# Carrying the sign of a weight through a leaky activation while float64 weights are converted

## The chip, the cores and the metric

The kernel runs on one core of a Trainium2 chip. The metric is the device time of one execution in microseconds (us), as the median of the runs shown. The engines are TensorE (PE, with its weight loads shown as PEld), VectorE (DVE), ScalarE (ACT), GpSimd (POOL) and the queues that start transfers, SyncE (SP) above all.

## The reference

Attention with a learned bias over positions (4 batches, 8 heads, 576 positions, head size 64) is followed by a feed-forward layer on 2304 tokens. The second part is the one that matters here:

```python
def _moe_ref(x, w_in, w_out):          # x: 2304 x 512, w_in: 512 x 2048, w_out: 2048 x 512
    h = x @ w_in
    beta = 1.0
    neg = h <= -beta
    pos = h >= beta
    g = np.where(pos, h, np.where(neg, 0.0, (h + beta) ** 2 / (4.0 * beta)))
    return (g @ w_out).astype(np.float32)
```

The two weight matrices arrive as float64. Everything else arrives as float32.

## The kernel before

Three stages follow each other. Stage one builds the position bias (the first third of the span). Stage two runs 16 steps of attention, one per pair of heads and batch; step 15 is the last. Stage three is the feed-forward layer, in three blocks of 768 tokens. A block runs over 16 slices f of the 2048 hidden columns, and each slice over two halves j of 384 tokens. For one slice and one half, `up_proj` issues 12 matmuls into a PSUM tile `h` (lines L731 to L733), `act` turns `h` into the gate (below), and `down_proj` issues 9 matmuls (L752 to L754) that add to six PSUM tiles `y`. There are two `h` tiles in all, so the up-projection two halves later writes into the tile that `act` has to have read.

`act` is a chain over three engines: VectorE clamps `h` into `c` (L740), ScalarE squares it (L741), VectorE takes the larger of `h` and `c` (L742), which frees the `h` tile, ScalarE rounds the result to `gh` (L743) and GpSimd forms the rest `gl` (L744). Values are kept as a high and a low part, since a product on TensorE takes shortened operands; hence three matmuls for each product.

During block 0 the weights are converted as well. Each slice has two tiles of 128 x 512 values, `wi` and `wo`, named `rawi`/`ai` and `rawo`/`ao` on the way, 32 tiles in all. `weight` does one: SyncE loads the 64-bit words into `raw` (L109); ScalarE turns the upper half of each word's low part into the three bits that float32 takes from it (L114, written back into `raw`); ScalarE scales the absolute value of the high part, read as a float32, by 2^-112 into `a` (L115), which rebases the exponent; VectorE shifts that left by three and joins the three bits (L116); VectorE masks the sign out of the high part and joins it (L117); ScalarE rounds to the high part of the weight (L119) and GpSimd forms the low part (L120). The `raw` buffer can be loaded again once its last reader is done, which is L117. From slice 2 on, all `wo` tiles take turns in one buffer and all `wi` tiles in two.

The tokens `x` of a half are loaded by eight transfers on SyncE (L438 twice, L447 six times, fewer where a piece is whole), then multiplied and split on VectorE and ScalarE (L461, L462, L463, L467). `xh0_1_1` below is token block 0, row group 1, half 1. Four such loads, for half 1 of block 0, stand between the attention and the feed-forward layer's full pace.

The order of the instructions on each engine is set when the program is built: a scheduler merges the stages from what it reckons each instruction costs, and every engine then works its list strictly in order. A waiting instruction holds up all that stands behind it on its engine. The functions print below with the profile's line numbers.

Of the kernel before, what the change touches and what calls it, by code (L numbers as in the profile page):

```python
# [8 lines left out]
F32 = mybir.dt.float32  # L9
# [3 lines left out]
AF = mybir.ActivationFunctionType  # L13
ALU = mybir.AluOpType
# [35 lines left out]
def attn_cpb_moe_kernel(ctx, tc, qk, vL, cb, win, wout, lw, dd, ident, ii, out):  # L50
    nc = tc.nc
# [42 lines left out]
    def raw_pool():  # L94
        turn[0] += 1
        return rps[turn[0] % len(rps)]
# [8 lines left out]
    def weight(src, dst, name):  # L105

        rp = raw_pool()
        raw = rp.tile([P, DM, 2], I32, tag="raw", name=f"raw{name}")
        nc.sync.dma_start(out=raw.rearrange("p a b -> p (a b)"), in_=src.bitcast(I32))  # L109
        a = rp.tile([P, DM], F32, tag="a", name=f"a{name}")  # L110
        t = a.bitcast(I32)
        lo, hi = raw[:, :, 0], raw[:, :, 1]

        nc.scalar.activation(lo, raw.bitcast(U16).rearrange("p a (b c) -> p a b c", c=2)[:, :, 0, 1], AF.Identity, scale=2.0**-13, bias=floor_s)  # L114
        nc.scalar.activation(a, hi.bitcast(F32), AF.Abs, scale=2.0**-112)  # L115
        nc.vector.scalar_tensor_tensor(out=t, in0=t, scalar=3, in1=lo, op0=ALU.logical_shift_left, op1=ALU.bitwise_or)  # L116
        nc.vector.scalar_tensor_tensor(out=t, in0=hi, scalar=-0x80000000, in1=t, op0=ALU.bitwise_and, op1=ALU.bitwise_or)  # L117
        h, l = dst
        nc.scalar.copy(h, t.bitcast(F32))  # L119
        nc.gpsimd.tensor_tensor(out=l, in0=t.bitcast(F32), in1=h.bitcast(F32), op=ALU.subtract)  # L120

    def weights(f):
        weight(win[f], [x.rearrange("p a b -> p (a b)") for x in wi[f]], f"i{f}")
        weight(wout[f * P : f * P + P], wo[f], f"o{f}")
# [752 lines left out]
```

## Time and profile before

| | us |
|---|---|
| median of 3 runs | 824.17 (823.49 to 824.81) |
| the profiled execution, whole | 826.46 |
| span of its trace | 824.7 |
| TensorE busy in the span | 733.7 (89%) |
| VectorE busy | 522.7 (63%) |
| ScalarE busy | 468.9 (57%) |
| GpSimd busy | 420.6 (51%) |

The trace starts at 0 and ends at 824.7; attention ends near 391, the weights are converted from 367 to 524, block 0 ends near 549. Busy shares over the whole span say little, since the stages have different limits; the rows further down are cut to the stretch in which the weights are converted. A row of a timeline gives the start, the length, the engine, the line and the tiles, and in brackets how long the engine had been idle before and what ended that. "PEclk" is the granted clock of TensorE, 1.00 being 2.4 GHz and 0.50 being 1.2 GHz.

### The profile page before, as it was taken

How to read it: one execution, taken by the hardware profiler on the slowest of the kernel's cores; microseconds unless marked ns; L12 is line 12 of the kernel's file. 1: busy time of each engine (PE TensorE's matmuls, PEld its weight loads, DVE VectorE, ACT ScalarE, POOL GpSimd, SP SyncE). 2: the span in 40 equal slices, each digit the busy share in tenths (PEclk: the TensorE clock that was granted, in tenths of full speed). 3: DMA queues.
4: the chain of work that ended last, by engine and by line, in shares of the span. 5: the costliest groups of instructions: out<-in, count | busy, mean ns of one | idle time of the engine just before them, and what ended most of it. 6: DMA issues, size and time to landing. Idle time of an engine off the chain costs nothing. (4 is left out here: it accounts for less than half of the span.)

```text
span 824.7 us, 13466 instructions
## 1 busy us (share of the span) xinstructions
PE 733.7 (89%) x4692; PEld 645.4 (78%) x4692; DVE 522.7 (63%) x1053; ACT 468.9 (57%) x1014; POOL 420.6 (51%) x385
## 2 busy tenths in 40 slices
PE   2766779899989999987499889999999999999998
PEld 1232579898989989976387778899999999999996
DVE  8999858788768888866598867366322234222222
ACT  1986758698878888777477854443222233222222
POOL 5875667778767878873176654422222222222221
PEclk9967989999999999998799999999999999999999
DMA  6676787866796587536654455035100012000002
GB/s 192 181 205 200 197 193 198 253 176 169 196 243 177 149 233 172 127 82 168 202 172 161 154 144 156 26 105 171 32 1 1 1 29 76 1 1 1 1 0 78
DMA packets 58660, 103.60 MB, mean 126 GB/s; under 512 B 12496, under 2 KB 32608, under 8 KB 58592
## 3 DMA queue, kind: packets, MB, share of 16 engines
q1 hardware_dynamic: 44976, 83.08, 35.2%
q0 software_dynamic: 2304, 9.96, 5.9%
q10 hardware_dynamic: 11312, 9.70, 3.8%
q8 instruction: 37, 0.61, 0.3%
q14 instruction: 31, 0.25, 0.1%
HBM read 67.63 MB, written 25.12 MB: 112 GB/s over the span
## 5 line engine op out<-in xcount | busy, mean ns | idle before, releaser
L744 POOL TENSOR_TENSOR gl<-c,gh 128x384 fp32r<-128x384 f32 x96 | 103.5, 1078 | 241.9 <-ACT gh L743 212.4
L731 PE MATMUL h<-xh,wi 128*128 128x384 f32 x384 | 133.7, 348 | 21.6 <-DVE c L742 13.8
L741 ACT ACTIVATE c<-c,half_s 128x384 f32<-128x384 f32 x96 | 59.1, 615 | 162.4 <-DVE c L740 162.4
L740 DVE TENSOR_SCALAR c<-h 128x384 f32<-128x384 f32 x96 | 53.2, 554 | 138.9 <-PE h L733 138.9
L732 PE MATMUL h<-xl,wi 128*128 128x384 f32 x384 | 131.5, 342 | 0.8 <-POOL xl L465 0.7
L733 PE MATMUL h<-xh,wi 128*128 128x384 f32 x384 | 131.6, 343 | 0.3 <-POOL wi L120 0.3
L558 POOL TENSOR_TENSOR lo<-c,hi 128x512 fp32r<-128x512 f32 x75 | 100.8, 1349 | 60.8 <-DVE hi L557 57.9
L754 PE MATMUL y<-wo,gl 128*128 128x512 f32 x288 | 114.0, 396 | 0.0
L753 PE MATMUL y<-wo,gh 128*128 128x512 f32 x288 | 113.7, 395 | 0.0
L752 PE MATMUL y<-wo,gh 128*128 128x512 f32 x288 | 112.0, 389 | 0.0
L511 DVE CUSTOM_DVE_ANT_0 e<-S,bias 128x576 f32<-128x576 f32 x128 | 93.9, 746 | 21.8 <-PE S L509 21.5
L518 ACT ACTIVATE e<-e,mx 128x576 f32<-128x576 f32 x128 | 99.7, 780 | 4.0 <-DVE mx L511 1.9
L731 PEld LDWEIGHTS h<-xh,wi 128*128 128x128 f32 x384 | 73.7, 192 | 32.8 <-DVE c L742 20.0
L508 PE MATMUL S<-kh,qa 128*128 128x288 f32 x256 | 80.2, 329 | 19.0 <-DMA kh<-kh 7.6
L742 DVE TENSOR_TENSOR c<-h,c 128x384 f32<-128x384 f32 x96 | 53.4, 556 | 52.4 <-ACT c L741 52.4
L743 ACT CAST gh<-c 128x384 fp32r<-128x384 f32 x96 | 49.2, 513 | 53.4 <-DVE c L742 50.9
L732 PEld LDWEIGHTS h<-xl,wi 128*128 128x128 f32 x384 | 73.8, 192 | 5.3 <-POOL xl L465 1.0
L573 PE MATMUL T<-id_s,e 128*128 128x128 f32 x512 | 73.3, 276 | 2.0 <-ACT e L518 1.4
L733 PEld LDWEIGHTS h<-xh,wi 128*128 128x128 f32 x384 | 73.6, 192 | 0.6 <-POOL wi L120 0.5
L509 PE MATMUL S<-ls,qa 128*128 128x288 f32 x256 | 73.0, 302 | 0.0
L508 PEld LDWEIGHTS S<-kh,qa 128*128 128x128 f32 x256 | 49.0, 191 | 26.9 <-DVE mx L511 11.5
L573 PEld LDWEIGHTS T<-id_s,e 128*128 128x128 f32 x512 | 61.2, 142 | 3.2 <-ACT e L518 1.7
(143 smaller groups left out, 1583.8 us busy)
## 6 DMA issues: line engine op xcount, KB each, us to landing
bias_d<-y SPq DMA_DIRECT2D x36, 295.5 KB, 3.2
qk<-in_qk_dram SPq DMA_DIRECT2D x16, 608.0 KB
qa<-in_qk_dram POOLq DMA_DIRECT2D x16, 608.0 KB, 6.6
x<-xT SPq DMA_DIRECT2D x48, 192.0 KB, 3.7
rawi<-in_win_dram SPq DMA_DIRECT2D x16, 512.0 KB, 3.8
rawo<-in_wout_dram SPq DMA_DIRECT2D x16, 512.0 KB, 4.1
v<-in_vL_dram SPq DMA_DIRECT2D x16, 320.0 KB, 3.2
qa<-ls SPq DMA_DIRECT2D x32, 152.0 KB, 3.8
```

The costliest lines, as they stand in the source:

```text
L508: nc.tensor.matmul(ps[:, hf, :HS], qs[:, qc], kh[:, kc : kc + HS], start=True, stop=False)
L511: nc.vector.tensor_tensor_reduce(out=ev.rearrange("p (a b) -> p a b", a=2), in0=ps[:, :, :HS], in1=bias[k][:, S * j : S * j + S].rearrange ...
L518: lambda ev=ev, j=j: nc.scalar.activation(ev, ev, AF.Exp, bias=mx[:, j : j + 1], scale=-1.0, accum_out=sm[:, 4 * j + k : 4 * j + k + 1])
L558: r = nc.gpsimd.tensor_tensor(out=lo, in0=m, in1=hi.bitcast(F32), op=ALU.subtract)
L573: nc.tensor.transpose(ps[:, tb, :], e[:, c0 : c0 + P], id_s)
L731: nc.tensor.matmul(ps[:, :TH], wh_, xh, start=k == 0, stop=False)
L732: nc.tensor.matmul(ps[:, :TH], wh_, xl, start=False, stop=False)
L733: nc.tensor.matmul(ps[:, :TH], wl_, xh, start=False, stop=k == NK - 1)
L744: nc.gpsimd.tensor_tensor(out=gl, in0=c, in1=gh.bitcast(F32), op=ALU.subtract)
L752: nc.tensor.matmul(y, gh[:, c], wo[f][0], start=f == 0, stop=False)
L753: nc.tensor.matmul(y, gh[:, c], wo[f][1], start=False, stop=False)
L754: nc.tensor.matmul(y, gl[:, c], wo[f][0], start=False, stop=f == NF - 1)
```

## The change

L115 becomes a leaky function: for a positive value it still gives the value times 2^-112, and for a negative one that times -(2^32), which is positive and has the exponent field raised by 32, one bit (bit 28) that is otherwise clear. The shift by three in L116 moves that bit to bit 31, the sign. L117 goes away, and with it 32 instructions on VectorE (1050 rows of its list become 1018). Nothing reads the high part of `raw` after L115, and L116 is the last reader of `raw`. Later lines move up by one (L742 is L741 in the changed program).

```diff
         nc.scalar.activation(lo, raw.bitcast(U16)..., AF.Identity, scale=2.0**-13, bias=floor_s)
-        nc.scalar.activation(a, hi.bitcast(F32), AF.Abs, scale=2.0**-112)
+        nc.scalar.activation(a, hi.bitcast(F32), AF.Prelu, scale=2.0**-112, alpha=-(2.0**32))
         nc.vector.scalar_tensor_tensor(out=t, in0=t, scalar=3, in1=lo, op0=ALU.logical_shift_left, op1=ALU.bitwise_or)
-        nc.vector.scalar_tensor_tensor(out=t, in0=hi, scalar=-0x80000000, in1=t, op0=ALU.bitwise_and, op1=ALU.bitwise_or)
         h, l = dst
```

Since the scheduler merges by cost, the lists of all engines change between the end of the attention and the last weight. TensorE's list has the same 4564 rows and differs in nine short places, all between the last attention step and slice 2 of block 0.

VectorE's list, in slices 3 and 4 of block 0 (`c4_0` is `c` of slice 4, half 0; `ai7` is weight tile `wi` of slice 7), before:

```order
L742 TENSOR_TENSOR c3_1_6210<-h3_1_6188,c3_1_6210 128x384
L117 SCALAR_TENSOR_TENSOR ai7_6328<-rawi7_6326,ai7_6328 128x512
L116 SCALAR_TENSOR_TENSOR ai8_6406<-ai8_6406,rawi8_6404 128x512
L117 SCALAR_TENSOR_TENSOR ai8_6406<-rawi8_6404,ai8_6406 128x512
L740 TENSOR_SCALAR c4_0_6240<-h4_0_6218 128x384
L116 SCALAR_TENSOR_TENSOR ao5_6181<-ao5_6181,rawo5_6179 128x512
L117 SCALAR_TENSOR_TENSOR ao5_6181<-rawo5_6179,ao5_6181 128x512
L742 TENSOR_TENSOR c4_0_6240<-h4_0_6218,c4_0_6240 128x384
```

The same place in the changed program:

```order
L741 TENSOR_TENSOR c3_1_6198<-h3_1_6176,c3_1_6198 128x384
L116 SCALAR_TENSOR_TENSOR ai7_6314<-ai7_6314,rawi7_6312 128x512
L739 TENSOR_SCALAR c4_0_6228<-h4_0_6206 128x384
L116 SCALAR_TENSOR_TENSOR ai8_6390<-ai8_6390,rawi8_6388 128x512
L741 TENSOR_TENSOR c4_0_6228<-h4_0_6206,c4_0_6228 128x384
```

Between the two joins of `c` (L742, now L741) six instructions became three: the three L117 are gone, and one L116 on either side moved past the joins.

SyncE's list, at the loads of the token half 1 of block 0 (`x0_0_1` and `x0_1_1`) and of the weights `rawi1` and `rawo1`, before:

```order
L447 DMA x0_0_1_5867<-rT0_1_75 64x192
L109 DMA rawi1_5702<-in_win_dram 128x1024
L447 DMA x0_0_1_5867<-rT0_1_75 64x192
L438 DMA x0_1_1_5882<-xT1_0_65 64x2x384 x2
L447 DMA x0_1_1_5882<-rT1_0_78 64x128 x2
L447 DMA x0_1_1_5882<-rT1_0_78 64x64 x2
L447 DMA x0_1_1_5882<-rT1_1_79 64x192
L109 DMA rawo1_5711<-in_wout_dram 128x1024
L447 DMA x0_1_1_5882<-rT1_1_79 64x192
```

The same place in the changed program:

```order
L109 DMA rawi1_5700<-in_win_dram 128x1024
L446 DMA x0_0_1_5863<-rT0_1_75 64x192 x2
L437 DMA x0_1_1_5878<-xT1_0_65 64x2x384 x2
L446 DMA x0_1_1_5878<-rT1_0_78 64x128 x2
L109 DMA rawo1_5708<-in_wout_dram 128x1024
L446 DMA x0_1_1_5878<-rT1_0_78 64x64 x2
L446 DMA x0_1_1_5878<-rT1_1_79 64x192 x2
```

The weight loads moved forward: behind `rawi1` stand two token loads of `x0_0_1` instead of one, and behind `rawo1` four of `x0_1_1` instead of one.

ScalarE's list, in slice 7, where the first tokens of block 1 are rounded (`xh768_0_0`), before:

```order
L119 CAST wi0_15_5860<-ai15_6952 128x512
L741 ACTIVATE c7_1_6522<-c7_1_6522,half_s_113 128x384
L463 CAST xh768_0_0_7039<-x768_0_0_7032 128x384
L743 CAST gh7_1_6523<-c7_1_6522 128x384
L114 ACTIVATE rawo10_6569<-rawo10_6569,floor_s_115 128x512
```

The same place in the changed program:

```order
L118 CAST wi0_15_5856<-ai15_6922 128x512
L118 CAST wo0_10_5838<-ao10_6550 128x512
L462 CAST xh768_0_0_7007<-x768_0_0_7000 128x384
L740 ACTIVATE c7_1_6502<-c7_1_6502,half_s_113 128x384
L742 CAST gh7_1_6503<-c7_1_6502 128x384
```

The square of `c7_1` moved from ahead of `xh768_0_0` to behind it.

## Rows read from the trace of the kernel before

**Rows 1.** The page's table of 40 slices, VectorE's busy tenths.

```profile
DVE  8999858788768888866598867366322234222222
```

**Rows 2.** Busy us of each engine by stretch: PE, PEld, DVE, ACT, POOL, PEclk, DMA.

```profile
400.00:440.00 40.00, 31.40 (x138) 27.36 (x139) 32.19 (x42) 27.08 (x48) 21.09 (x16) 0.83 0.56 179
440.00:480.00 40.00, 34.78 (x161) 29.83 (x160) 31.75 (x40) 28.19 (x50) 28.84 (x21) 0.96 0.46 149
480.00:525.00 45.00, 41.47 (x203) 35.95 (x203) 31.25 (x50) 24.85 (x44) 20.29 (x18) 1.00 0.49 138
560.00:824.70 264.70, 260.67 (x1304) 235.30 (x1302) 83.16 (x146) 75.32 (x135) 62.77 (x62) 1.00 0.09 27
```

**Rows 3.** TensorE's waits, 396 to 409, 409 to 480, 480 to 525: us, times, longest.

```profile
PE h L731 <- ACT xh L463: 6.7, 2, 3.5
...
PE h L731 <- DVE c L742: 8.6, 7, 3.1
...
PE h L731 <- DVE c L742: 3.5, 4, 2.2
```

**Rows 4.** VectorE's timeline, 409 to 411 and 436 to 443.5.

```profile
409.74 0.68 DVE L117 SCALAR_TENSOR_TENSOR ai<-rawi,ai 128x512 int32<-128x512 int32 x1
...
436.59 0.55 DVE L742 TENSOR_TENSOR c<-h,c 128x384 f32<-128x384 f32 x1
437.06 0.68 DVE L117 SCALAR_TENSOR_TENSOR ai<-rawi,ai 128x512 int32<-128x512 int32 x1
437.66 0.68 DVE L116 SCALAR_TENSOR_TENSOR ai<-ai,rawi 128x512 int32<-128x512 int32 x1
438.37 1.40 DVE L117 SCALAR_TENSOR_TENSOR ai<-rawi,ai 128x512 int32<-128x512 int32 x1
439.69 0.55 DVE L740 TENSOR_SCALAR c<-h 128x384 f32<-128x384 f32 x1
440.16 1.32 DVE L116 SCALAR_TENSOR_TENSOR ao<-ao,rawo 128x512 int32<-128x512 int32 x1
441.52 1.64 DVE L117 SCALAR_TENSOR_TENSOR ao<-rawo,ao 128x512 int32<-128x512 int32 x1
443.08 0.54 DVE L742 TENSOR_TENSOR c<-h,c 128x384 f32<-128x384 f32 x1
```

**Rows 5.** TensorE's timeline at 443.68.

```profile
443.68 0.69 PE L731 MATMUL h<-xh,wi 128*128 128x384 f32 x1 [2.02 <-DVE c L742]
```

**Rows 6.** TensorE alone, 444 to 447: busy us, PEclk, DMA.

```profile
444.00:447.00 3.00, 3.00 (x10) 0.50 0.51 175
```

**Rows 7.** L117 alone on VectorE, by stretch: busy us (count), PEclk, DMA.

```profile
400.00:480.00 80.00, 24.49 (x22) 0.89 0.51 164
480.00:525.00 45.00, 5.65 (x6) 1.00 0.49 138
```

**Rows 8.** ScalarE's groups: busy us, mean ns of one, idle before.

```profile
L518 ACT ACTIVATE e<-e,mx 128x576 f32<-128x576 f32 x128 | 99.7, 780 | 4.0 <-DVE mx L511 1.9 <-DMA v<-in_vL_dram 0.9 <-ACT ai L115 0.7
...
L548 ACT CAST hi<-T 128x512 fp32r<-128x512 f32 x53 | 29.0, 580 | 6.9 <-PE S_L L530 4.9 <-PE T L573 2.0
...
L115 ACT ACTIVATE ai<-rawi 128x512 f32<-128x512 f32 x16 | 10.7, 668 | 0.0
...
L239 ACT ACT_TABLE_LOAD x1 | 1.3, 1283 | 4.9 <-DMA lw_s<-in_lw_dram 4.9
```

**Rows 9.** SyncE's timeline at the two weight loads.

```profile
383.12 0.34 SPq L109 DMA_DIRECT2D rawi<-in_win_dram  x1
...
390.27 0.33 SPq L109 DMA_DIRECT2D rawo<-in_wout_dram  x1
390.64 0.44 SPq L447 DMA_DIRECT2D x<-rT  x1
```

**Rows 10.** L120 on GpSimd, 405 to 525: duration ns min/median/max.

```profile
L120 POOL TENSOR_TENSOR wi<-ai,wi x14: 1270/1470/1843, 411.4 to 478.9; 128x512 fp32r<-128x512 f32 x14
```

**Rows 11.** ScalarE's timeline at the first tokens of block 1.

```profile
480.17 0.51 ACT L463 CAST xh<-x 128x384 fp32r<-128x384 f32 x1 [2.24 <-POOL wi L120]
```

## The prediction

> **What bounds the kernel now.** I read the table of slices first, then cut the span into stretches. After 560 TensorE is busy 260.67 of 264.70 us [rows 2]: nothing that VectorE does there can shorten the time, and no conversion is left there. From 400 to 480 it is another engine's turn: VectorE is busy 32.19 and 31.75 of 40 us, while TensorE stands idle 8.6 and 5.2 us and ScalarE and GpSimd are lighter than both [rows 2]. The page shows the same hump in VectorE's slices 18 to 23 [rows 1]. What TensorE waits for there is one thing: the join of `c` on VectorE (L742), 8.6 us in seven waits from 409 to 480 and 3.5 us in four waits from 480 to 525. Ahead of that, 6.7 us in two waits go to the tokens of half 1 [rows 3].
>
> Why the join is late is seen in one gap. TensorE starts at 443.68 after 2.02 us idle [rows 5]. VectorE had run without a pause from 436.59: between two joins stand L117, L116, L117, the clamp, L116, L117 [rows 4]. Three of the six are L117, and they hold 0.68, 1.40 and 1.64, together 3.7 us, more than the gap. So L117 lies on the path here, though it belongs to weights that are needed only slices later.
>
> **The change, part by part.** *L117 leaves VectorE.* From 400 to 480 that is 22 instructions and 24.49 us, from 480 to 525 six and 5.65 us [rows 7]. VectorE's load from 400 to 480 falls from 63.9 to 39.4 of 80 us [rows 2, 7]. That is an engine's time, not the kernel's: only what ends in a TensorE gap counts. Four terms follow.
>
> First, the gap before 410.94, the longest of the seven with 3.1 us [rows 3]. The join there stands behind one L117 of 0.68 [rows 4]; the rest is the chain from a late matmul through clamp and square. Credit 0.7.
>
> Second, the other six waits up to 480: 8.6 - 3.1 = 5.5 us. In the changed list the place of the 443.68 gap keeps only two L116 and the clamp between the joins, so 3.7 us leave against 2.02 of gap, and this gap should close. Not every gap will, since lists in order jar also without a full engine. The nearest measure is 480 to 525, where VectorE is busy 31.25 of 45 us [rows 2], with three waits of 3.5 - 2.2 = 1.3 us beside the long one [rows 3]. At that rate the 68 us from 412 to 480 keep 1.3 / 39 x 68 = 2.3 us. Credit 5.5 - 2.3 = 3.2; bounds 0 and 5.5.
>
> Third, the clock. Right after the 2.02 us gap TensorE ran at 0.50, the lower of its two levels, for the 3 us from 444 to 447 [rows 6], which is 1.5 us of work lost. If the gap closes, so should that dip. Credit 1.5; bounds 0 and 1.5.
>
> Fourth, 480 to 525: 3.5 us in four waits. The long one, 2.2, starts with ScalarE, which waited 2.24 us to round `xh768_0_0` until GpSimd was done with the last `wi` tile [rows 11]. The changed list keeps that wait, and even puts the square of `c7_1` behind it; I credit it one L117 of 0.68 and no more. The other three are 1.3 us, and an L117 there lasts 5.65 / 6 = 0.94 us [rows 7]; I credit half, 0.7. Together 1.4; bounds 0 and 3.5.
>
> *L115 becomes a leaky function.* The trace of before has no such operation. ScalarE's rows on tiles of this kind lie between 580 ns (a rounding of 512 columns) and 780 ns (the exponential, 576 columns); the absolute value takes 668 [rows 8]. It keeps its place and its scale, so I take the 668 of the nearest row, no change. The ends are -0.09 and +0.11 us a tile, times 22 tiles -2 and +2.5 us on ScalarE, which is busy 55.3 of 80 us [rows 2] and has room for either. It costs nothing under the time in which TensorE works; if ScalarE filled up, it would cost its whole length (a rival below).
>
> *The raw buffer is free one instruction earlier.* Before, SyncE could start the next load only behind L117; now behind L116. So weights come earlier, which speeds nothing by itself, as TensorE never waits for a `wo` in these rows [rows 3]. *Queues are shifted by that.* SyncE started `rawi1` at 383.12 and `rawo1` at 390.27 [rows 9], each after an L117. Now each can start up to one L117 earlier (0.68 to 1.64 [rows 4]), but two and four token loads stand behind them instead of one and one. One such issue takes 0.44 [rows 9] and they follow each other: with `rawo1` 1.6 us earlier and three loads more behind it (3 x 0.44 = 1.3, more where an issue is slower) `x0_1_1` is complete at about the same time as before. If `rawo1` doesn't start earlier, the tokens slip by 1.3 to 2 us and TensorE's second token wait grows by as much. I take 0; bounds -0.8 and +2.
>
> *One rule of contention.* The same L117 on the same shapes takes 0.68 at 437.06 and 1.64 at 441.52 [rows 4], and GpSimd's L120 takes 1.27 to 1.84 [rows 10]. The Trainium skill (SBUF — State Buffer, Who interferes with whom) says why: a VectorE instruction with two SBUF inputs contends with a GpSimd instruction that reads SBUF, through a shared port that one of them holds. The trace agrees in that the lengths spread up to 2.4 times. By that rule, L116 and L120 would get shorter as well when half of the two-input instructions go. By the rows that is up to 0.57 us per `wi` tile on GpSimd, which is on no gap's path here; the sum is the same without it.
>
> The sum against the profiled execution: 0.7 + 3.2 + 1.5 + 1.4 = 6.8 us, 826.46 - 6.8 = 819.7. The profiled execution is 2.3 us above the median of 824.17, so the forecast for the median is 824.17 - 6.8 = **817.4 us**. Next in line is then TensorE itself, with the two token waits of 6.7 us unchanged.
>
> **The rivals.**
> - *All gaps close.* 0.7 + 5.5 + 1.5 + 3.5 = 11.2 gives 813.0. For it: 24.49 us leave VectorE against 5.5 of gap. Against: the wait of `xh768_0_0` stays.
> - *ScalarE takes VectorE's place.* Its list carries three conversions per tile and two steps of `c`, 55.3 us of 80 [rows 2], and each `wo` load still waits for its only buffer; a ScalarE that waits for a raw load holds up the square behind it. Then half of the second term remains and the dip too: 0.7 + 2.75 gives 3.5, 820.7. For it: ScalarE would be 55.3 of some 73 us, with waits on top. Against: it was lighter than VectorE in every stretch.
> - *Nothing comes of it.* The scheduler has filled the freed places with other conversions, the joins come as late as before: 824.2. For it: the lists did move everywhere. Against: the place in slices 3 and 4.
> - *Slower: the leaky function is dear.* It would sit on ScalarE, 22 times from 400 to 480. VectorE bound that stretch at 63.9 of 80 us, so ScalarE would from (63.9 - 55.3) / 22 = 0.39 us more per tile, that is from a length of 1.06 us. At double the absolute value, 1.34 us, ScalarE has 55.3 + 14.7 = 70 us of work; at VectorE's share of 0.8 the stretch takes 87.5 us, 7.5 more: 831.7. Against it: no row of that size exceeds 0.78 [rows 8].
> - *The table must be switched.* Before, one table load of 1.283 us stands at the start [rows 8]; the changed program's list also has just one, at the same place. Two loads a tile would be 2.57 x 32 = 82 us on ScalarE, and some 40 us or more of that in the time. The Trainium skill (ScalarE: Activation LUTs, Table sets: the hidden batching unit) warns of this: a function outside the loaded set needs a switch of about 2.66 us. The one load in the list makes the chance very small, and it is counted with the last rival.
>
> **How the numbers follow.** Chances: forecast 0.50 (815 to 819.5, counting a token slip of 2 us), all gaps close 0.13, ScalarE takes over 0.20, nothing 0.10, slower 0.07. The range of 8 in 10 takes in the first three and their bounds: 812.8 to 823.0; it leaves out most of "nothing" and the slower side. A change of 0.2%, 1.65 us, is about what a measurement of this kernel can tell from none. Faster by more: 0.50 + 0.13 + 0.20 = 0.83; within: 0.10; slower by more: 0.07.
>
> **What would show it.** Right: the leaky function at 0.64 to 0.70 us; VectorE at about 40 of 80 us from 400 to 480; TensorE's waits for the join from 409 to 480 down from 8.6 to about 5 (3.1 - 0.7 + 2.3); no 0.50 clock after a gap near 443; the two token waits still near 6.7. Wrong, if the token waits grow by several us, if TensorE's waits for the join stay while VectorE itself is waiting for ScalarE's squares, or if the leaky function lasts over 1 us.

## The result and the profile after

The kernel after takes **815.29 us** in the median (814.53 to 815.77, 4 runs) against 823.83 for the kernel before in the same runs (822.76 to 824.81, 4 runs): ratio 0.9896, interval 0.9879 to 0.9913, so 8.5 us less. The forecast was 817.4 us with a range of 812.8 to 823.0. The profiled execution took 815.15 us, its span is 813.4.

VectorE's slices of the page after, beside [rows 1]: from slice 18 on the row is lower, and the hump ends earlier.

```profile
DVE  8999868788768888866475566276322243222222
```

Busy us of each engine by stretch (PE, PEld, DVE, ACT, POOL, then PEclk, DMA share, GB/s), the same cuts as [rows 2]:

```profile
400.00:440.00 40.00, 34.01 (x156) 30.70 (x157) 23.87 (x36) 32.50 (x58) 25.76 (x20) 0.87 0.66 216
440.00:480.00 40.00, 37.59 (x177) 32.76 (x176) 23.98 (x34) 30.20 (x55) 26.92 (x22) 0.96 0.54 168
480.00:525.00 45.00, 44.70 (x225) 39.94 (x224) 24.17 (x38) 18.76 (x33) 17.04 (x15) 1.00 0.29 83
```

VectorE's 63.9 of 80 us are 47.9 now, TensorE's 66.2 are 71.6, and ScalarE went from 55.3 to 62.7. The last of these is no dearer instruction: with the joins earlier, more tiles and more steps of `c` lie in the same 80 us (25 conversions in place of 22, 17 clamps in place of 15).

TensorE's waits (us in total, times, longest), 396 to 409, 409 to 480 and 480 to 525, beside [rows 3]:

```profile
PE h L730 <- ACT xh L462: 5.3, 2, 3.9
PE h L730 <- DVE c L741: 2.2, 1, 2.2
...
PE h L730 <- DVE c L741: 2.4, 1, 2.4
...
PE h L730 <- DVE c L741: 0.2, 1, 0.2
```

Before, the join cost 8.6 + 3.5 = 12.1 us in eleven waits; now 2.2 + 2.4 + 0.2 = 4.8 us in three. The gap that stood at 410.94 stands at 407.59, 2.18 us long. The other six up to 480 are gone, the one at 443.68 with them [rows 5]. This is one execution; a second profile of the same kernel, further down, has small waits there again. The two that are left in TensorE's timeline behind it:

```profile
469.89 0.45 PE L730 MATMUL h<-xh,wi 128*128 128x384 f32 x1 [2.39 <-DVE c L741]
...
501.54 0.45 PE L730 MATMUL h<-xh,wi 128*128 128x384 f32 x1 [0.23 <-DVE c L741]
```

The first does not start on VectorE. Its chain, in the timelines of ScalarE and of VectorE: ScalarE waits 1.43 us to round the first tokens of block 1 (`xh768_0_0`), the square of `c` comes behind that, VectorE splits off the tokens' low part (1.07) and only then joins.

```profile
467.75 0.51 ACT L462 CAST xh<-x 128x384 fp32r<-128x384 f32 x1 [1.43 <-POOL wi L119]
468.17 0.61 ACT L740 ACTIVATE c<-c,half_s 128x384 f32<-128x384 f32 x1
...
468.30 1.07 DVE L466 TENSOR_TENSOR xl<-x,xh 128x384 fp32r<-128x384 f32 x1 [2.23 <-ACT xh L462]
469.29 0.55 DVE L741 TENSOR_TENSOR c<-h,c 128x384 f32<-128x384 f32 x1
```

It is the wait of [rows 11], which the prediction expected to stay. And the clock falls behind it, where it had fallen behind 443.68 before [rows 6]; all engines, 470 to 476:

```profile
470.00:472.00 2.00, 2.00 (x10) 2.00 (x11) 0.31 (x1) 1.66 (x3) 1.01 (x1) 0.77 0.62 188
472.00:474.00 2.00, 2.00 (x7) 1.81 (x6) 1.73 (x4) 1.14 (x2) 0.89 (x1) 0.50 0.31 63
474.00:476.00 2.00, 2.00 (x10) 1.65 (x9) 0.61 (x2) 0.79 (x2) 1.47 (x2) 0.88 0.91 297
```

The leaky function, in ScalarE's groups (busy us, mean ns of one, idle before), beside L115 in [rows 8]:

```profile
L115 ACT ACTIVATE ai<-rawi 128x512 f32<-128x512 f32 x16 | 10.6, 661 | 0.0
L115 ACT ACTIVATE ao<-rawo 128x512 f32<-128x512 f32 x16 | 10.5, 654 | 0.0
```

661 ns on `wi` tiles against the 668 of the absolute value, and still one table load in the program.

### The profile page after: what moved, and what is told of

Its sections match the earlier page's. It is cut to its first block, busy times and chain, and to the rows that moved or that the text cites. A ratio compares the mean times of both kernels' runs of the same rounds, so it can differ in the third digit from the quotient of the medians.

```text
span 813.4 us, 13433 instructions
## 1 busy us (share of the span) xinstructions
PE 732.9 (90%) x4692; PEld 645.8 (79%) x4692; DVE 499.6 (61%) x1021; ACT 467.2 (57%) x1014; POOL 418.3 (51%) x385
## 5 line engine op out<-in xcount | busy, mean ns | idle before, releaser
L741 DVE TENSOR_TENSOR c<-h,c 128x384 f32<-128x384 f32 x96 | 53.3, 556 | 50.3 <-ACT c L740 50.3
L742 ACT CAST gh<-c 128x384 fp32r<-128x384 f32 x96 | 49.2, 512 | 51.2 <-DVE c L741 50.1
```

## The experiments

The theory: L117 held VectorE between two joins, and the gain is VectorE's time from 400 to 525, no more and no less. Rivals: the gain comes from the raw buffer, which is free one instruction earlier; from the other order of the lists, which moved everywhere; or the leaky function has a price that eats part of a larger gain.

### The operation back, without its effect

```diff
 # the kernel after
         nc.vector.scalar_tensor_tensor(out=t, in0=t, scalar=3, in1=lo, ...)
+        nc.vector.scalar_tensor_tensor(out=t, in0=hi, scalar=0, in1=t, op0=ALU.bitwise_and, op1=ALU.bitwise_or)
```

> The leaky function stays, and behind the join a third-operand instruction is put back on VectorE that reads the high part of raw, masks it with 0 and joins that: same shape and operands as the old L117, no effect on the values. The lists of all engines are then row for row those of the kernel before. Theory (VectorE's time delays the joins of c): back to the time before, 823.8 within 1.5 us, the leaky function as long as the absolute value (0.65 to 0.67 us). Rival, the leaky function itself is cheaper or dearer in a way that shows in the time: 1.65 us or more away from the time before.

Measured: 824.61 us (820.57 to 827.11, 10 runs), ratio 1.0008 (0.9982 to 1.0034): the time of before. In this kernel the two waits of 2.02 and 2.10 us are back, at 442.21 and 483.89 of TensorE's timeline:

```profile
442.21 0.45 PE L731 MATMUL h<-xh,wi 128*128 128x384 f32 x1 [2.02 <-DVE c L742]
...
483.89 0.44 PE L731 MATMUL h<-xh,wi 128*128 128x384 f32 x1 [2.10 <-DVE c L742]
```

With the leaky function kept, the one VectorE instruction takes the whole gain away. The order of the lists is here the one of before, so this run alone doesn't part VectorE's time from the order, nor from the raw buffer.

### The same on the tile alone

The no-effect operation reads `t` twice (and with all ones, or with itself), so that L116 stays the last reader of `raw` and the buffer is free as early as in the kernel after.

```diff
+        nc.vector.scalar_tensor_tensor(out=t, in0=t, scalar=-1, in1=t, op0=ALU.bitwise_and, op1=ALU.bitwise_or)
```

> As the kernel after, with an instruction put back on VectorE that has no effect and reads only the tile a (twice), not raw: VectorE's time is that of before, raw is free one instruction earlier as after. Theory (VectorE's time): near the time before, 821 to 825. Rival (the gain is the earlier free raw buffer): near the time after, 815 to 817.

Measured: 825.99 us (822.88 to 828.46, 10 runs), ratio 1.0020 (0.9999 to 1.0041), 1 us above the range of the theory and far from that of the rival. VectorE's load is not quite that of before, but 68.8 of 80 us (busy us by stretch, as above). One more tile lies in the stretch, and the operation that reads the tile twice is longer: 1195 ns on the `wi` tiles, against 966 for L117 there before.

```profile
400.00:440.00 40.00, 31.07 (x138) 26.79 (x138) 31.77 (x41) 27.40 (x49) 23.14 (x17) 0.87 0.58 190
440.00:480.00 40.00, 33.23 (x153) 28.09 (x152) 37.05 (x42) 30.02 (x54) 30.14 (x21) 0.96 0.49 154
```

With the buffer free as early as in the kernel after, nothing of the gain is left, so the raw buffer is not its source. That the release is worth a little, which the longer operation takes back, is not ruled out.

The rival of the order is narrowed, not closed. The lists of this kernel are neither those of before nor those of after, and it is as slow as the two programs with the lists of before; a new order, with VectorE as full, gave nothing here. No run keeps the order of the kernel after and gives VectorE its old load.

### The kernel before without L117, absolute value kept

L115 stays the absolute value and L117 is taken out, so the sign of the weights is left out of the computation.

```diff
 # the kernel before
-        nc.vector.scalar_tensor_tensor(out=t, in0=hi, scalar=-0x80000000, in1=t, op0=ALU.bitwise_and, op1=ALU.bitwise_or)
```

> The kernel before with L117 taken out and the absolute value kept; it leaves out the signs of the weights, so its values are others. All lists are row for row those of the kernel after. Theory: 815.3 within 1.2 us, since the leaky function costs what the absolute value costs. Rival (the leaky function has a price hidden in the 815.3): 814 or less.

Measured: 815.43 us (811.88 to 816.35, 4 runs), ratio 0.9882 (0.9852 to 0.9912), against 0.9896 (0.9879 to 0.9913) for the kernel after. The lists are row for row those of the kernel after. The two can't be told apart: the leaky function in place of the absolute value has no price that these runs show, though by the intervals one of 2 us could hide.

### A short operation in its place

The no-effect operation of the first experiment on 32 of the 512 columns.

```diff
 # the kernel after
+        nc.vector.scalar_tensor_tensor(out=t[:, :32], in0=hi[:, :32], scalar=0, in1=t[:, :32], ...)
```

> As the kernel after, with the no-effect instruction that reads raw put back on 32 of 512 columns: VectorE has as many instructions as before and raw is held as long, but each lasts some 0.1 to 0.2 us instead of 0.7 to 1.6. Its lists are neither those of before nor those of after. Theory (the time on VectorE counts): 815 to 818. Rival (the number of instructions, the held buffer, or the order that the build makes): 820 to 824.

Measured: 820.70 us (816.47 to 824.71, 10 runs), ratio 0.9958 (0.9931 to 0.9986). This misses the theory's 815 to 818 and lies in the rival's range. The instruction was not as short as expected, in VectorE's groups:

```profile
L117 DVE SCALAR_TENSOR_TENSOR ai<-rawi,ai 128x32 int32<-128x32 int32 x16 | 9.5, 597 | 0.2
```

One sixteenth of the columns lasts 597 ns in the mean (175 the shortest, 1181 the longest), against 930 for the whole tile in the first experiment. So VectorE got back only part: 54.5 of 80 us from 400 to 480, against 47.9 without the operation and 63.9 before.

```profile
400.00:440.00 40.00, 33.88 (x159) 30.25 (x160) 28.16 (x45) 29.96 (x54) 22.35 (x18) 0.87 0.62 202
440.00:480.00 40.00, 34.32 (x165) 28.78 (x164) 26.35 (x43) 29.65 (x54) 26.17 (x21) 1.00 0.50 161
```

The time stands between the two as VectorE's load does: (63.9 - 54.5) / (63.9 - 47.9) = 0.59 of the load, and by the medians 3.3 of 8.5 us = 0.39 of the gain. The profiled execution took 818.22, which is 5.8 us under the median of before, 0.68 of the gain; the ten runs spread over 8.2 us. So the direction is the theory's, and whether time and load go in step can't be told from this. What the expectation mis-sized is the price of a short instruction. As the number of instructions and the hold on the buffer are those of before and the order is a third one, this run doesn't part the theory from the rival.

### The operation twice

The other direction: one more operation per tile than before.

```diff
 # the kernel before
         nc.vector.scalar_tensor_tensor(out=t, in0=hi, scalar=-0x80000000, in1=t, ...)
+        nc.vector.scalar_tensor_tensor(out=t, in0=t, scalar=-1, in1=t, op0=ALU.bitwise_and, op1=ALU.bitwise_or)
```

> The kernel before with one more no-effect VectorE operation per tile behind L117 (and with all ones, or the tile itself: the value stays). Nothing is left out of the computation. Theory (the gain is VectorE's time in 400 to 525 us): the operation lasts 0.60 to 0.70 us, so 400 to 480 would want about 64 + 20 = 84 us of VectorE in 80 us; it is full, the waits of TensorE for VectorE's weight tiles grow well over their 8.6 us, and the time is 830 to 845 us. Rival (VectorE's time doesn't matter, only the order or the raw tile's release does): 822 to 826 us. A time of 827 to 829 us would say that VectorE has slack left that its busy share doesn't show.

Measured: 839.40 us (838.48 to 839.98, 4 runs), ratio 1.0173 (1.0156 to 1.0190): 14.6 us more. VectorE is full; its busy us by stretch, and TensorE's waits from 409 to 480:

```profile
400.00:440.00 40.00, 29.53 (x128) 24.41 (x126) 35.02 (x43) 24.37 (x42) 19.30 (x14) 0.87 0.49 161
440.00:480.00 40.00, 31.97 (x141) 27.77 (x141) 39.93 (x46) 25.60 (x43) 24.23 (x17) 0.91 0.39 130
```

```profile
PE h L732 <- DVE c L743: 14.3, 9, 2.8
```

From 440 to 480 VectorE stands still for 0.07 us. Taking one instruction away gave 8.5 us, adding one costs 14.6: with VectorE at its limit the same instruction counts for more.

### No VectorE work on the weights at all

L116 is taken out too: the shift, and by that the sign's place, and the three low bits are left out.

```diff
 # the kernel after
-        nc.vector.scalar_tensor_tensor(out=t, in0=t, scalar=3, in1=lo, op0=ALU.logical_shift_left, op1=ALU.bitwise_or)
```

> The kernel after without the joining operation L116 as well, so VectorE has no operation on a weight tile at all; the shift by two places, the sign's place and the three low bits are left out, and the weights are wrong by that. Theory (after the change VectorE no longer sets the time; one wait of 2.4 us for the token tile xh768_0_0 is what is left): little more to gain, 812 to 815.5 us, with the wait near 470 us still there. Rival (VectorE still binds in 400 to 525 us, where it is busy 47.9 of 80 us): a gain like that of the change itself, 809 us or less.

Measured: 812.69 us (808.70 to 813.43, 4 runs), ratio 0.9839 (0.9813 to 0.9865). By the medians that is 2.6 us under the kernel after, by the ratios 4.7, and 1.0 under the next kernel below, which was measured with it. VectorE falls to 26.1 of 80 us, by more than the first time, and gives about half of what the first instruction gave at most: it is no longer what bounds the stretch.

```profile
400.00:440.00 40.00, 33.69 (x156) 30.60 (x157) 12.78 (x23) 32.78 (x60) 23.37 (x21) 0.87 0.67 216
440.00:480.00 40.00, 38.10 (x183) 33.97 (x183) 13.29 (x24) 33.18 (x61) 28.68 (x24) 0.96 0.63 193
```

What is late next shows at the wait that is left near 470, in the timelines of TensorE, ScalarE and VectorE: ScalarE stands 3.89 us for the raw `wo` of a late slice to arrive, and the square that the join needs is queued behind its conversion. An add on tokens, itself late by its load, stands ahead of the join on VectorE and ends last, 0.3 us behind the square.

```profile
472.83 0.45 PE L729 MATMUL h<-xh,wi 128*128 128x384 f32 x1 [1.90 <-DVE c L740]
...
470.80 0.75 ACT L114 ACTIVATE rawo<-rawo,floor_s 128x512 int32<-128x512 uint16 x1 [3.89 <-DMA rawo<-in_wout_dram]
471.44 0.60 ACT L739 ACTIVATE c<-c,half_s 128x384 f32<-128x384 f32 x1
...
471.75 0.56 DVE L459 TENSOR_TENSOR x<-x 128x384 f32<-128x384 f32 x1 [3.41 <-DMA x<-xT]
```

### The wait that is left: the tokens queued later

The rounding of `xh768_0_0` is queued on ScalarE behind the square of slice 9's first half.

```diff
 # the kernel after; sq[f, j] is the square at L740
-    split_x(blk + TB, k, 0)
+    if blk == 0 and k == 0:
+        with tc.issue_after(sq[9, 0].ins):
+            split_x(blk + TB, k, 0)
+    else:
+        split_x(blk + TB, k, 0)
```

> The kernel after with one conversion of the next token block (xh768_0_0, L462) queued on ScalarE behind the square of slice 9's first half, in place of ahead of it. Nothing is left out. Theory (the last wait of TensorE, 2.39 us at 469.89 us, is ScalarE held up by that conversion, which waits for POOL and a DMA; the clock of 0.50 behind the wait costs some 1.5 us more): both go, 811 to 813.5 us, and no clock of 0.50 in 440 to 525 us. Rival (the wait only moves to the next square or to another clock dip): 814.5 to 816 us.

Measured: 813.65 us (812.39 to 815.59, 4 runs), ratio 0.9863 (0.9842 to 0.9883), which overlaps the interval of the kernel after; the median lies between the ranges of theory and rival. In its profile, whose execution took 815.59, the wait at 469.89 is gone, and three others stand in TensorE's timeline, 2.5 us together as before:

```profile
475.07 0.44 PE L730 MATMUL h<-xh,wi 128*128 128x384 f32 x1 [1.41 <-DVE c L741]
...
488.42 0.44 PE L730 MATMUL h<-xh,wi 128*128 128x384 f32 x1 [0.53 <-DVE c L741]
497.73 0.45 PE L730 MATMUL h<-xh,wi 128*128 128x384 f32 x1 [0.55 <-DVE c L741]
```

So it was measured once more, beside the kernel after on the same chip.

> The kernel after as it stands, beside the same with the later token conversion, so that these two are compared against one another on one chip. Expected of both theories: 815 us, 814 to 816, with one wait for xh768_0_0's square of 2 to 2.5 us near 470 us and a clock of 0.50 behind it.

> The kernel after with the conversion of xh768_0_0 queued behind the square of slice 9's first half, again, with more rounds. Theory (what it gives is the clock: in its first profile the waits of 2.6 us became three of 1.41, 0.53 and 0.55 us, no shorter together, but none was followed by a clock of 0.50): 1 to 2 us under the kernel after on this chip. Rival (it only moves the wait, and run-to-run scatter made the difference): within 0.8 us of it.

Measured: the kernel after 816.48 us (809.18 to 819.35, 6 runs), ratio 0.9900 (0.9861 to 0.9939); the tokens later 815.94 (814.74 to 816.61, 5 runs), ratio 0.9905 (0.9880 to 0.9929). The two differ by 0.5 us, as the rival has it, and the 813.65 did not come again.

The kernel after came out 0.5 us above its expected range, and its profile, of an execution of 817.05, is not that of the first. The wait near 470 is there, 2.57 us long, but no clock of 0.50 behind it, and small waits stand around it in TensorE's timeline:

```profile
452.17 0.45 PE L730 MATMUL h<-xh,wi 128*128 128x384 f32 x1 [1.30 <-DVE c L741]
472.04 0.45 PE L730 MATMUL h<-xh,wi 128*128 128x384 f32 x1 [2.57 <-DVE c L741]
489.88 0.45 PE L730 MATMUL h<-xh,wi 128*128 128x384 f32 x1 [0.71 <-DVE c L741]
503.40 0.44 PE L730 MATMUL h<-xh,wi 128*128 128x384 f32 x1 [0.23 <-DVE c L741]
```

VectorE is as busy as in the first profile, 47.3 of 80 us. So the small waits come and go from one execution to the next at the same load: 1.30 + 0.71 + 0.23 = 2.24 us here, 0.23 there. At the first of them VectorE was not full but stood idle itself, for ScalarE's square:

```profile
451.56 0.56 DVE L741 TENSOR_TENSOR c<-h,c 128x384 f32<-128x384 f32 x1 [1.39 <-ACT c L740]
```

With the tokens later the join is late for another reason. In VectorE's timeline of this second run an add on the tokens stands ahead of it, which waits for its load and takes 1.33:

```profile
472.32 1.33 DVE L460 TENSOR_TENSOR x<-x 128x384 f32<-128x384 f32 x1 [0.61 <-DMA x<-xT]
473.58 0.55 DVE L741 TENSOR_TENSOR c<-h,c 128x384 f32<-128x384 f32 x1
```

Taking one conversion of the tokens of block 1 out of its place only showed the next piece of work on tokens. Neither of these runs beats the kernel after by more than can be measured.

### The runs in one table

| kernel | VectorE, 400 to 480 (of 80 us) | TensorE's waits for the join, last token wait to 525 | median us |
|---|---|---|---|
| no VectorE work on weights | 26.1 | 6.3 | 812.69 |
| absolute value, no sign | 47.0 | 5.6 | 815.43 |
| after | 47.9 | 4.8 | 815.29 |
| after, again | 47.3 | 7.0 | 816.48 |
| tokens later | 50.5 | 4.7 | 813.65 |
| tokens later, again | 49.0 | 4.0 | 815.94 |
| short operation | 54.5 | 9.4 | 820.70 |
| before | 63.9 | 12.1 | 823.83 |
| operation without effect | 63.9 | 13.3 | 824.61 |
| the same on the tile alone | 68.8 | 12.7 | 825.99 |
| operation twice | 75.0 | 19.3 | 839.40 |

VectorE's load is the sum of the first two rows of the stretches, the waits are those that end in the two windows. Each row has one profile, and the medians come from four sets of runs, whose medians of before lie between 823.83 and 824.79. From about 50 to 75 us the time rises with VectorE's load, and steeply at the end; below that it hardly falls. The 6.3 us of the first row are two waits: the one of 1.90 shown above, and one of 4.4 right behind the tokens, at 407.44, a place where the kernel after waits 2.2. There the square starts at 406.20, behind the conversions of two weight tiles in ScalarE's list.

## Why the prediction was right, and where its terms were off

**The cause** was named rightly: L117 in VectorE's queue between the joins. Put back without its effect, it brings back the whole time (0.1% from before); taken from the kernel before without the leaky function, it gives the whole gain. The forecast was 2.1 us above the measured median. The size of the sum was partly luck, as the terms show.

**First term, the gap before 410.94.** Credited 0.7; it went from 3.06 to 2.18, so 0.9. As the prediction had it, the rest is the chain from a late matmul.

**Second and fourth term, the other ten waits.** Credited 3.2 + 1.4 = 4.6 of 9.06 us; in the profiled execution 6.4 went (9.06 - 2.39 - 0.23), and the upper bound for the second term, 5.5, was what happened. In the second profile of the same kernel 4.25 went (9.06 - 2.57 - 2.24). The prediction let 2.9 us of small waits stay (2.3 up to 480, 0.6 behind); 0.23 stayed in the one execution and 2.24 in the other. So the term was 1.8 too small in one and 0.35 too large in the other, and two profiles can't tell which is the rule. VectorE's share doesn't decide it: 0.60 (400 to 480) and 0.54 (480 to 525) in the first, 0.59 and 0.58 in the second. The wait of `xh768_0_0` stayed, as forecast, and moved ahead of 480; the 0.68 credited on it was wrong in both, since it went from 2.17 to 2.39 and 2.57. The sign of about 5 us of waits up to 480 came out as 2.18 + 2.39 = 4.6 and as 6.0, with other parts than forecast.

**Third term, the clock.** Credited 1.5. The fall behind 443.68 went, but in the profiled execution one behind 469.89 came, and 440 to 480 has the mean of 0.96 that it had before: nothing was gained there. In the second profile there is no fall from 440 to 525, and the 1.5 came. The kernel before is no steadier: the run of the operation without effect has its lists, row for row, and a gap of the same 2.02 us at 442.21, and its clock from 440 to 480 is 1.00. A fall that one trace shows is a matter of that execution as much as of the kernel.

**The sum.** It came near because one term too small and one too large offset each other in the profiled execution, 0.9 + 6.4 + 0 = 7.3 us; in the second profile they are close to their credits, 0.9 + 4.25 + 1.5 = 6.65, against 6.8. From the matmul that ends the last token wait to the end of the span it is 418.4 us before (824.7 - 406.29) and 409.6 after (813.4 - 403.81), and 409.6 again in the second profile (815.3 - 405.69), so 8.8 us less both times. The terms leave 1.5 and 2.1 of it. In the first profile that isn't the clock, though the mean from 400 to 440 rose from 0.83 to 0.87: the slow time that went there was idle. TensorE's busy time in each us times what the granted clock lacks to 1.00, added up over the stretch, is 5.1 us before, 5.2 after and 2.3 in the second profile. So in the second 1.3 of the 2.1 is clock beyond the third term; the rest, 1.5 and 0.8, no run takes apart. Against the profile of the operation without effect, whose join waits are 13.2 us from the gap at 409.19 on, 8.4 us of waits went, and its stretch is 8.2 longer.

**The leaky function** at 661 ns is where the prediction put it, and the "dear function" rival (from 1.06 us on) is out. The rule that a function of a table set that isn't loaded needs one more table load (the Trainium skill, ScalarE: Activation LUTs, Table sets: the hidden batching unit) found no use here: one load stands in the trace, as before.

**VectorE at 40 of 80 us** was wrong: 47.9. The 24.5 us of L117 left, but 8.4 came: three more L116 (25.1 us in place of 21.9), two more pairs of clamp and join, and tokens of block 1 earlier. A stretch with fixed ends isn't the same work once the work moves.

**The token chain** was taken at 0: from a transpose of the attention's last step (372.40 in TensorE's timeline before, 369.69 after) to the matmul that ends the last token wait (406.29 and 403.81) it is 33.9 us before and 34.1 after. The two waits are 5.3 against 6.7 us; a third, of 0.60, stands ahead of them at 394.30.

**"ScalarE takes VectorE's place"** had some of it right: ScalarE is the busiest engine beside TensorE from 400 to 480 now, the wait of 1.30 in the second profile stands behind its square, and in the run without VectorE's work its list holds the square back at both waits, 4.4 and 1.90. But in the kernel after the waits up to 480 other than the gap behind the tokens and that of `xh768_0_0` were 0 and 1.30 us, not half of the second term (2.75).

**The rule of contention** (the Trainium skill, SBUF — State Buffer, Who interferes with whom: a VectorE instruction with two SBUF inputs contends with a GpSimd instruction that reads SBUF) was left out of the sum. From 405 to 525 the weight tiles' subtraction on GpSimd went from 1507 to 1386 ns a `wi` tile (1419 in the second profile), as the rule has it, and to 1298 where VectorE does no two-input work on weights at all. On `wo` tiles it hardly moved: 1354, then 1342 (1369), and 1302 without that work. L116 did not get shorter: 955 to 1090 ns (1053) on `wi`, 910 to 921 (937) on `wo`. So what got shorter is GpSimd's work on `wi` tiles; which of the two engines waits for the other, and what decides it, no run here tells.

## What to carry to other kernels

Where an engine that works its list in order is busy for most of a stretch (here 0.80) and the consumer's waits all end at one of its instructions, look at what stands between two of these. One instruction less per tile took 7.3 of 12.1 us of waits in one execution and 5.1 in another; the largest that survived had another cause, which its own chain names. Count the cost of an edit against the engine that has slack (here ScalarE's existing operation, which carries the sign for nothing that could be measured), and stop once the waits name another resource: the second instruction less gave 1.0 to 4.7 us after 8.5. A sum of terms that comes out right can hide two errors, so compare it gap by gap, and in more than one execution: here two of them disagree on the small waits and on the clock, and agree on the whole.

## What the runs showed of the hardware

- A VectorE operation on 32 columns of a `wi` tile that L116 has written lasted 597 ns in the mean (175 to 1181), against 930 (671 to 1782) for the same on 512 columns. A sixteenth of the columns saved a third of the length. Whether the rest is a wait for an instruction ahead of it or for GpSimd was not separated.
- TensorE's clock did not fall by the length of the idle time alone. It fell to 0.50 behind gaps of 2.39 us in the kernel after and of 1.86 in the second run with the tokens later, and did not behind one of 2.57 when the kernel after was run again. Two gaps of the same 2.02 us, in programs with the same lists, had a fall behind them in one [rows 6] and none in the other, whose row is the last. The rows (all engines, then PEclk), the gap of 1.86 first, then that of 2.57:

```profile
472.00:474.00 2.00, 0.32 (x2) 0.00 (x0) 1.68 (x2) 0.42 (x1) 1.25 (x1) 1.00 0.74 226
474.00:476.00 2.00, 1.82 (x9) 1.82 (x10) 1.07 (x3) 1.29 (x3) 1.01 (x1) 0.84 0.83 248
476.00:478.00 2.00, 2.00 (x7) 1.87 (x6) 1.69 (x4) 2.00 (x5) 0.00 (x0) 0.50 0.37 96
```

```profile
470.00:472.00 2.00, 0.00 (x0) 0.00 (x0) 1.54 (x2) 0.94 (x2) 1.10 (x1) 1.00 0.46 142
472.00:474.00 2.00, 1.96 (x11) 1.96 (x12) 0.16 (x1) 1.73 (x3) 1.03 (x1) 1.00 0.77 213
474.00:476.00 2.00, 2.00 (x11) 1.70 (x10) 1.73 (x4) 1.14 (x2) 0.74 (x1) 1.00 0.30 67
```

```profile
440.00:480.00 40.00, 33.54 (x162) 28.77 (x162) 30.80 (x40) 28.57 (x51) 27.83 (x21) 1.00 0.45 142
```

A forecast can't credit one such fall in full: another gap may bring it back, as in the first profile here, and the next execution of the same lists may not have it.
